# Differences of products 7 and 4 written over their source, and four x operands of the middle groups split in the next stage

## The chip, the cores and the metric

The kernel runs on one core of one Trainium2 chip. Its engines have a queue of instructions each and meet through semaphores: TensorE (PE, matmuls), VectorE (DVE), ScalarE (ACT), GpSimd (POOL) and SyncE (SP, which issues most transfers). The metric is the device time of one execution in microseconds (us); lower is better.

## What is computed

```python
def reference(q, k, v, w_in, w_out):          # q, k, v: 8 x 12 x 448 x 64
    scores = q @ k.transpose(0, 1, 3, 2) / sqrt(64) - log(448)
    a = sigmoid(scores) @ v
    x = a.transpose(0, 2, 1, 3).reshape(3584, 768)
    r = maximum(x @ w_in, 0)                  # w_in: 768 x 2048
    return (r * r) @ w_out                    # w_out: 2048 x 768
```

Everything is float32. Each matmul operand is split in two parts of 32 bits that TensorE takes (fp32r): a high part h, and what is left of the value, the low part l. A product is the sum of three matmuls, h by h, h by l and l by h.

## The kernel before

The attention comes first (to about 236 us). Then the two GEMMs run on the tokens in four groups g = 0 to 3 (WIDTHS: two halves of 512, 512, 512 and 256 tokens each). In each group both GEMMs work by Winograd's form of Strassen's method: a 2x2 block product by seven products of sums, numbered 1 to 7, in place of eight.

**First GEMM** (`gemm1`). A step (n, i) is product n of column block i (of 8), nine matmuls of 128x512. The order of steps is a table: group 0 starts with LEAD, the others go by ROUNDS; all end with TAIL. Products 1, 6, 5 and 3 of a block run on in one PSUM bank ("ha"), 7 and 4 in a second ("hb"), and 2 in a third ("hc"). Product 6 adds to the bank of product 1, so ACT must first copy product 1 out of it: `snap`, L757, tiles "s". By ROUNDS the first steps of a group are (1,0), (2,0), (6,0), (7,0).

The x operands of the next group are made at steps of the second GEMM that the table NEXT_X names, in its products 5, 4 and 3: loads, sums on DVE (L439), and the split by `split_to`, a cast on ACT (L382, "x1h") and a subtraction on DVE (L384, "x1l"). Of 768 rows of x a tile holds 512, and a second one ("y") 256.

**Second GEMM** (`gemm2`). Products come in the order 1, 2, 6, 7, 5, 4, 3, each over four blocks j of the hidden dimension. While a product runs, `operand(n, j)` makes the operands of the next one: a sum on DVE in place (L831 for product 7 in the tile "g11", L834 for product 4 in "g21") and the split in o7_g_j h and l, or o4. In groups 1 and 2, products 2, 7 and 4 are done by the same seven-product method once more. Their operand needs four differences of 128x256 quarters, made by POOL (L846 to L849) in a fresh tile d7_g_j (`differences_of`), which `split_to` then splits in d7_g_j h and l. In names, `d7_1_3l` is product 7, group 1, block 3, low part; the trace leaves numbers in the middle out and shows `d_3l`. For one block PE runs 21 matmuls of 128x256 (L883, "oq") and six of 128x512 ("ob").

What sets the order: attention and the first GEMM of group 0 are in the order in which they are written. From there on a tile scheduler orders each engine's instructions in the build, on all engines at once, and on the chip each engine goes through its own in that order. The pool "op2" has 32 tiles of 128x1024, and all of g, o, d and most x are taken from it.

Of the kernel before, what the change touches and what calls it, by code (L numbers as in the profile page):

```python
# [10 lines left out]
F32R = mybir.dt.float32r  # L11
# [4 lines left out]
ALU = mybir.AluOpType  # L16
# [12 lines left out]
NG = B // 2  # L29
# [11 lines left out]
NG = len(WIDTHS)  # L41
# [28 lines left out]
STEPS = LEAD + [s for s in ROUNDS if s not in LEAD] + TAIL, ROUNDS + TAIL  # L70
# [10 lines left out]
    (4, 4): ("t1", "t2"),  # L81
    (4, 6): (6,),
    (3, 0): ("t3",),
    (3, 1): (7,),
    (3, 3): (5,),
    (3, 5): (3,),
    (3, 6): ("t4",),
    (3, 7): (4,),
}

ORDERS = [(n, i) for n in ORDER for i in range(NI)]
LAST = ORDER[-1], -1
# [3 lines left out]
Q = WIDE // 2  # L96
# [15 lines left out]
def sigmoid_attention_relu2_mlp(  # L112
# [48 lines left out]
    nc = tc.nc  # L161
# [3 lines left out]
    def flat2(name, dtype=F32):  # L165
        return sb.tile([P, 2 * WIDE], dtype, tag="op2", bufs=N2, name=name)
# [9 lines left out]
    def blocks_of(name, n, dtype=F32):  # L176
        return flat2(name, dtype).rearrange("p (a s) -> p a s", s=n)
# [203 lines left out]
    def split_to(hi, lo, raw, later=None):  # L381
        nc.scalar.copy(out=hi, in_=raw)  # L382
        if later is None:
            nc.vector.tensor_sub(out=lo, in0=raw, in1=hi.bitcast(F32))  # L384
        else:
            later.append(lambda: nc.vector.tensor_sub(out=lo, in0=raw, in1=hi.bitcast(F32)))
# [16 lines left out]
    def split_or_joint(raw, name, n):  # L403
        return joint(raw, name, 2 * WIDE // n, n) if n < WIDE else split(raw, name, n)
# [77 lines left out]
    x, vt, xs, at, pav, xo, f64, w = {}, {}, {}, {}, {}, {}, {}, {}  # L482
# [156 lines left out]

    def order_of(g, m):  # L640
        if m == 0:
            return STEPS[g > 0]
        return ORDERS if g < NG - 1 else [*ORDERS[:-NI], LAST]

    sequence = [(g, m, n, i) for g in range(NG) for m in range(2) for n, i in order_of(g, m)]

    def units_of(g, m, n, i):
# [167 lines left out]
    def gemm2(g, blocks, operands1):  # L815
# [3 lines left out]
        ops, t2 = {1: operands1}, {}  # L819
        twice = TWICE if g in TWICE_IN else ()  # L820
        differences = {}

        def operand(n, j):

            if n == 6:
                t2[j] = blocks_of(f"gt2_{g}_{j}", n_tok)
                nc.vector.tensor_sub(out=t2[j], in0=blocks["22", j], in1=blocks["12", j])  # L827
                raw = t2[j]
            elif n == 7:
                raw = blocks["11", j]  # L830
                nc.vector.tensor_sub(out=raw, in0=t2[j], in1=raw)  # L831
            elif n == 4:
                raw = blocks["21", j]
                nc.vector.tensor_sub(out=raw, in0=raw, in1=t2[j])  # L834
            else:
                raw = blocks[{2: "21", 5: "12", 3: "22"}[n], j]
            ops.setdefault(n, {})[j] = split_or_joint(raw, f"o{n}_{g}_{j}", n_tok)
            if n in twice:
                differences[n, j] = differences_of(raw, f"d{n}_{g}_{j}")

        def differences_of(raw, name):

            t, hi, lo = flat2(name), flat2(name + "h", F32R), flat2(name + "l", F32R)
            t1, t2, t3, t4 = (t[:, k * Q : k * Q + Q] for k in range(4))
            b11, b12, b21, b22 = (raw[:, k, h * Q : h * Q + Q] for k in range(2) for h in range(2))
            nc.gpsimd.tensor_tensor(out=t1, in0=b12, in1=b11, op=ALU.subtract)  # L846
            nc.gpsimd.tensor_tensor(out=t2, in0=b22, in1=t1, op=ALU.subtract)
            nc.gpsimd.tensor_tensor(out=t3, in0=b22, in1=b12, op=ALU.subtract)
            nc.gpsimd.tensor_tensor(out=t4, in0=b21, in1=t2, op=ALU.subtract)  # L849
            split_to(hi, lo, t)  # L850
            return hi, lo

        def products(n, j):

            unit = g, 1, j, n
            w, s, d = loaded[unit], summed[unit], differences[n, j]

            def block(e, k):
                return tuple(t[:, k, e * P : e * P + P] for t in w)

            def total(k):
                return tuple(t[:, k * P - P : k * P] for t in s)

            def part(k, h):
                return tuple(t[:, k, h * Q : h * Q + Q] for t in ops[n][j])

            def difference(k):
                return tuple(t[:, k * Q - Q : k * Q] for t in d)

            operands = {  # L870
                2: (block(0, 1), part(1, 0)),
                3: (total(4), part(1, 1)),
                4: (block(1, 1), difference(4)),
                5: (total(1), difference(1)),
                1: (block(0, 0), part(0, 0)),
                6: (total(2), difference(2)),
                7: (total(3), difference(3)),
            }
            for k, ((wh, wl), (xh, xl)) in operands.items():
                at, half = SUMS_AT[k]  # L880
                out = banks["q", at][:, half * Q : half * Q + Q]
                for c, (a, b) in enumerate(((wh, xh), (wh, xl), (wl, xh))):
                    nc.tensor.matmul(  # L883
                        out, a, b, start=j == 0 and c == 0 and half == 0, stop=j == NI // 2 - 1 and c == 2,
                        skip_group_check=True,
                    )
# [71 lines left out]
        def run(n, places):  # L958
            parts = []
            for i, e in places:  # L960
                w = tuple(t[:, i % 2].rearrange("p (c m) -> p c m", m=P) for t in loaded[g, 1, i // 2, n])
                operand = ops[n][i // of]
                x = tuple(t[:, i % of] for t in operand) if n_tok == WIDE else operand[i % of]
                out, first, end = banks[CHAIN[n], e], n in (1, 7, 2) and i == 0, i == NI - 1
                if n_tok < WIDE and (n, e) == (ORDER[-1], NE - 1):
                    out, x = out[:, :n_tok], (x[:, :n_tok], x[:, n_tok:])
                parts.append((out, w, e, x, first, end))
            if isinstance(parts[0][3], tuple):
                for part in parts:
                    product(*part)  # L970
            else:
                side_by_side(parts)
            for i, e in places:
                if i == NI - 1:
                    finish(n, e)
# [19 lines left out]
        def step(n, at):  # L995
            k, i = CHAIN[n], at
            if n in twice:
                if i == 0:
                    for e in range(4):
                        banks["q", e] = bank(f"oq{n}_{g}_{e}", WIDE, 3 if e < 2 else None)  # L1000
                    if n != 4:
                        banks[k, NE - 1] = bank(f"o{k}_{g}", WIDE)
                j = i // 2
                if i == 2 * j:
                    products(n, j)
                else:
                    for c in range(2):
                        w = tuple(t[:, c].rearrange("p (c m) -> p c m", m=P) for t in loaded[g, 1, j, n])
                        x = tuple(t[:, c] for t in ops[n][j])
                        product(banks[k, NE - 1], w, NE - 1, x, n != 4 and (j, c) == (0, 0), (j, c) == (NI // 2 - 1, 1))  # L1010
                if i == NI - 1:
                    finish_twice(n)
                after = ORDER.index(n) + 1
                if after < len(ORDER) and i % of == 0:
                    operand(ORDER[after], i // of)
                return
# [11 lines left out]
            if after < len(ORDER) and i % of == 0:  # L1028
                operand(ORDER[after], i // of)
# [3 lines left out]
    def run_steps(begin, end, between):  # L1033
        for at in range(begin, end):
            g, m, n, i = sequence[at]
            if (m, n, i) == (0, *order_of(g, 0)[0]):
                made[g] = gemm1(g, ops[g])
            if (m, n, i) == (1, *ORDERS[0]):
                step, blocks, operands, done = made[g]
                done()  # L1040
                second[g] = gemm2(g, blocks, operands)
            (second[g] if m else made[g][0])(n, i)
            for piece in between.get(at, ()):
                piece()
            for piece, unit in stream.get(at, ()):
                piece(unit)
            if m and g < NG - 1:
                if (n, i) == next(iter(NEXT_X)):
                    ops[g + 1], next_x[g] = x_operands(g + 1)
                for name in NEXT_X.get((n, i), ()):  # L1050
                    next_x[g][name]()

    made, second, next_x = {}, {}, {}

# [95 lines left out]
```

## Time and profile before

| | |
|---|---|
| median of three runs | 1070.48 us (1066.46 to 1071.03) |
| profiled execution | 1069.48 us, its span 1067.7 us |
| mean granted TensorE clock | 0.995 |
| busy: PE, DVE, ACT, POOL | 1051.8, 835.4, 687.9, 241.7 us |

The span goes from the first to the last instruction; the execution's own time is 1.8 us longer. The view of the waits tells for how long an engine stood still, and which engine's instruction ended that. The timeline tells where it stood. In a timeline the microseconds of an instruction are from its start to its end, whatever holds it up in between.

### The profile page before, as it was taken

The numbers are of one execution on the slowest core, as the hardware profiler recorded it, in microseconds if no ns is written. First come the engines' busy times: TensorE is split into PE (matmuls) and PEld (weight loads), VectorE is DVE, ScalarE is ACT, GpSimd is POOL, SyncE is SP. The second block draws the span as 40 slices with busy tenths as digits, with TensorE's granted clock in tenths as the row PEclk, the third lists the DMA queues.
The fourth block names the chain that finished last, engine by engine and source line by source line (L and its number), as shares of the span: only waits on it lengthen the run. The fifth ranks groups of instructions, "written<-read, shape, count | busy, mean of one in ns | idle before, by whom it ended". The sixth has DMA issues, their size and how long they took to land.

```text
span 1067.7 us, 17202 instructions
## 1 busy us (share of the span) xinstructions
PE 1051.8 (99%) x6418; PEld 821.5 (77%) x6418; DVE 835.4 (78%) x1045; ACT 687.9 (64%) x960; POOL 241.7 (23%) x188
## 2 busy tenths in 40 slices
PE   9999999999999999999999999989999999999998
PEld 4555555557888888877888888878888887889987
DVE  5999998977768899793555698894556689877897
ACT  7998998877667855663334647473344647567863
POOL 1322231300222344300000639300002559100000
PEclk9999999999999999998999999999999999999999
DMA  9999999983666787983334868862336778775662
GB/s 363 395 371 392 335 404 361 336 286 116 214 208 207 245 285 241 331 297 116 102 91 140 297 205 298 288 230 75 103 96 218 251 258 286 258 242 165 203 209 69
DMA packets 121874, 255.93 MB, mean 240 GB/s; under 512 B 11712, under 2 KB 63680, under 8 KB 121792
## 3 DMA queue, kind: packets, MB, share of 16 engines
q1 hardware_dynamic: 121648, 254.79, 69.7%
q8 instruction: 50, 0.82, 0.3%
q14 instruction: 32, 0.26, 0.1%
q10 hardware_dynamic: 144, 0.07, 0.0%
HBM read 193.46 MB, written 61.34 MB: 239 GB/s over the span
## 4 chain that ended last, share of the span: by engine, by line
PE 81%; DVE 9%; DMA 3%; ACT 2%; POOL 2%; issue 2%; SPq 0%; ACTq 0%; DVEq 0%; POOLq 0%
PE ha L626 20%; PE oa L626 14%; PE pav L356 11%; PE hb L626 9%; PE sc L325 9%; PE hc L626 4%; PE oq L883 3%; PE ob L626 3%; PE oc L626 2%; DMA w<-w 2%; PE sr L341 2%; PE pav L368 2%; DVE w L384 1%; POOL d L846 1%; DVE gt L827 1%
## 5 line engine op out<-in xcount | busy, mean ns | idle before, releaser
L384 DVE TENSOR_TENSOR w<-w 128x768 fp32r<-128x768 f32 (+1 forms) x164 | 148.5, 913 | 95.7 <-ACT w L382 82.1
L382 ACT CAST w<-w 128x768 fp32r<-128x768 f32 (+1 forms) x165 | 127.0, 778 | 82.4 <-DMA w<-w 78.8
L313 ACT ACTIVATE at<-sc 128x896 f32<-128x896 f32 x144 | 119.3, 941 | 3.8 <-PE sc L325 3.7
L356 PE MATMUL pav<-at,v 64*64 64x448 f32 x1152 | 118.1, 540 | 0.0
L846 POOL TENSOR_TENSOR d<-g 128x256 f32<-128x256 f32 x24 | 33.6, 1400 | 339.2 <-PE ha L626 283.7
L215 POOL TENSOR_TENSOR a<-a,f 128x768 int32<-128x768 int32 x24 | 52.8, 2201 | 159.4 <-DVE a L212 94.0
L356 PEld LDWEIGHTS pav<-at,v 64*64 64x64 f32 x1152 | 41.6, 133 | 60.8 <-issue 53.5
L757 ACT COPY s<-ha 128x512 f32<-128x512 f32 (+1 forms) x64 | 34.0, 533 | 81.9 <-PE ha L626 77.8
L592 DVE TENSOR_TENSOR ql<-x,qh 128x896 fp32r<-128x896 f32 x46 | 67.9, 1516 | 0.0
L690 ACT CAST w<-w 128x768 fp32r<-128x768 f32 x56 | 46.7, 834 | 29.6 <-DMA w<-w 29.6
L325 PE MATMUL sc<-qh 64*128 64x448 f32 x282 | 53.9, 379 | 0.0
L325 PE MATMUL sc<-ql,qh 64*128 64x448 f32 x282 | 51.3, 360 | 0.0
L325 PE MATMUL sc<-qh,ql 64*128 64x448 f32 x282 | 51.0, 358 | 0.0
L378 DVE TENSOR_TENSOR xo<-pav,xo 128x448 f32<-128x448 f32 x48 | 29.5, 621 | 25.2 <-ACT xo L374 25.0
L626 PE MATMUL ha<-x_1h,w 128*128 128x512 f32 x128 | 45.7, 398 | 3.0 <-ACT s L757 3.0
L626 PE MATMUL ha<-x_2h,w 128*128 128x512 f32 x128 | 45.7, 398 | 2.8 <-ACT s L757 2.8
L215 POOL TENSOR_TENSOR b<-b,fd 128x384 int32<-128x384 int32 x16 | 20.4, 1278 | 118.8 <-ACT w L382 56.9
L626 PE MATMUL oa<-o_0h,w 128*128 128x512 f32 x144 | 46.3, 389 | 0.0
L626 PE MATMUL oa<-o_1h,w 128*128 128x512 f32 x144 | 46.3, 389 | 0.0
L626 PE MATMUL oa<-o_2h,w 128*128 128x512 f32 x144 | 46.3, 389 | 0.0
L626 PE MATMUL oa<-o_3h,w 128*128 128x512 f32 x144 | 46.3, 389 | 0.0
L626 PE MATMUL ha<-x_0h,w 128*128 128x512 f32 x128 | 44.8, 390 | 0.0
(575 smaller groups left out, 3057.0 us busy)
## 6 DMA issues: line engine op xcount, KB each, us to landing
w<-w SPq DMA_DIRECT2D x192, 384.0 KB, 3.7
w<-h SPq DMA_DIRECT2D x56, 384.0 KB, 5.6
x<-qk SPq DMA_DIRECT2D x47, 448.0 KB, 6.2
f<-w_in SPq DMA_DIRECT2D x16, 768.0 KB, 8.7
v<-v SPq DMA_DIRECT2D x24, 448.0 KB, 6.6
xd<-xo SPq DMA_DIRECT2D x48, 224.0 KB, 4.8
h<-w SPq DMA_DIRECT2D x28, 384.0 KB, 4.3
w<-s SPq DMA_DIRECT2D x48, 192.0 KB, 7.2
```

The source lines that it names most:

```text
L215: nc.gpsimd.tensor_tensor(out=wb, in0=wb, in1=t.bitcast(I32)[:, :, 0], op=ALU.add)
L313: nc.scalar.activation(at, sc, AF.Sigmoid, bias=NEG_LOG_S, scale=SCALE)
L325: nc.tensor.matmul(sc[:, j], x[kp][rows, 1, ks], x[qp][rows, 0], start=(n == 0), stop=(n == len(passes) - 1),)
L356: nc.tensor.matmul(sums[columns, h], vt[rows, n % 2 * NT + t, columns], at[t][rows, j], start=(t == 0 and (n % 2, h) != (1, 1)), stop=(t = ...
L382: nc.scalar.copy(out=hi, in_=raw)
L384: nc.vector.tensor_sub(out=lo, in0=raw, in1=hi.bitcast(F32))
L592: nc.vector.tensor_sub(out=xs[n][1], in0=x[n], in1=xs[n][0].bitcast(F32))
L626: nc.tensor.matmul(out, a[:, c], b, start=first and n == 0, stop=last and n == 2, skip_group_check=True)
L690: nc.scalar.copy(out=hi, in_=hi.bitcast(F32))
L757: nc.scalar.copy(out=s, in_=banks[chain, i])
L846: nc.gpsimd.tensor_tensor(out=t1, in0=b12, in1=b11, op=ALU.subtract)
L883: nc.tensor.matmul(out, a, b, start=j == 0 and c == 0 and half == 0, stop=j == NI // 2 - 1 and c == 2, skip_group_check=True,)
```

## The change

There are two parts.

First, `differences_of` gets an argument `spent`. For products 7 and 4 it is true: the four differences are written over their own source, the tile g11 (product 7) or g21 (product 4), and no fresh tile d is taken. The order is now t1, t3, t2, t4, and they lie in the tile as t1, t3, t4, t2, so that each is written where the source is no longer needed; `difference(k)` picks them accordingly. Since the source is overwritten, POOL's first write to a block now has to come after both instructions that read that block for the split: ACT's cast o7_g_j h and DVE's subtraction o7_g_j l. Each of the four POOL instructions now follows the one before it. Product 2 keeps its fresh tile.

Second, in groups 1 and 2 the steps of the first GEMM take the order of group 0: (1,0), (2,0), (1,1), (2,1), (6,0), (7,0), (6,1), (5,0), (7,1), (3,0) and so on. Their x operands 7, 5, 3 and 4 (with the sum t4 for the last) are now made at steps 0, 1, 3, 5 and 6 of this order (EARLY_X), no longer in product 3 of the second GEMM before. Group 3 keeps its order and the old places (LATE_X).

```diff
@@ -81,12 +81,9 @@
     (4, 4): ("t1", "t2"),
     (4, 6): (6,),
     (3, 0): ("t3",),
-    (3, 1): (7,),
-    (3, 3): (5,),
-    (3, 5): (3,),
-    (3, 6): ("t4",),
-    (3, 7): (4,),
 }
+EARLY_X = {0: (7,), 1: (5,), 3: (3,), 5: ("t4",), 6: (4,)}
+LATE_X = {(3, 1): (7,), (3, 3): (5,), (3, 5): (3,), (3, 6): ("t4",), (3, 7): (4,)}
 
 ORDERS = [(n, i) for n in ORDER for i in range(NI)]
 LAST = ORDER[-1], -1
@@ -639,7 +636,7 @@
 
     def order_of(g, m):
         if m == 0:
-            return STEPS[g > 0]
+            return STEPS[g == NG - 1]
         return ORDERS if g < NG - 1 else [*ORDERS[:-NI], LAST]
 
     sequence = [(g, m, n, i) for g in range(NG) for m in range(2) for n, i in order_of(g, m)]
@@ -836,18 +833,20 @@
                 raw = blocks[{2: "21", 5: "12", 3: "22"}[n], j]
             ops.setdefault(n, {})[j] = split_or_joint(raw, f"o{n}_{g}_{j}", n_tok)
             if n in twice:
-                differences[n, j] = differences_of(raw, f"d{n}_{g}_{j}")
-
-        def differences_of(raw, name):
-
-            t, hi, lo = flat2(name), flat2(name + "h", F32R), flat2(name + "l", F32R)
-            t1, t2, t3, t4 = (t[:, k * Q : k * Q + Q] for k in range(4))
-            b11, b12, b21, b22 = (raw[:, k, h * Q : h * Q + Q] for k in range(2) for h in range(2))
+                differences[n, j] = differences_of(raw, f"d{n}_{g}_{j}", n != 2)
+
+        def differences_of(raw, name, spent):
+
+            hi, lo = flat2(name + "h", F32R), flat2(name + "l", F32R)
+            flat = raw.rearrange("p k s -> p (k s)")
+            to = flat if spent else flat2(name)
+            b11, b12, b21, b22 = (flat[:, n * Q : n * Q + Q] for n in range(4))
+            t1, t3, t4, t2 = (to[:, n * Q : n * Q + Q] for n in range(4))
             nc.gpsimd.tensor_tensor(out=t1, in0=b12, in1=b11, op=ALU.subtract)
+            nc.gpsimd.tensor_tensor(out=t3, in0=b22, in1=b12, op=ALU.subtract)
             nc.gpsimd.tensor_tensor(out=t2, in0=b22, in1=t1, op=ALU.subtract)
-            nc.gpsimd.tensor_tensor(out=t3, in0=b22, in1=b12, op=ALU.subtract)
             nc.gpsimd.tensor_tensor(out=t4, in0=b21, in1=t2, op=ALU.subtract)
-            split_to(hi, lo, t)
+            split_to(hi, lo, to)
             return hi, lo
 
         def products(n, j):
@@ -865,7 +864,8 @@
                 return tuple(t[:, k, h * Q : h * Q + Q] for t in ops[n][j])
 
             def difference(k):
-                return tuple(t[:, k * Q - Q : k * Q] for t in d)
+                at = (1, 3, 4, 2).index(k) * Q
+                return tuple(t[:, at : at + Q] for t in d)
 
             operands = {
                 2: (block(0, 1), part(1, 0)),
@@ -1049,6 +1049,11 @@
                     ops[g + 1], next_x[g] = x_operands(g + 1)
                 for name in NEXT_X.get((n, i), ()):
                     next_x[g][name]()
+                for name in LATE_X.get((n, i), ()) if g == NG - 2 else ():
+                    next_x[g][name]()
+            if m == 0 and 0 < g < NG - 1:
+                for name in EARLY_X.get(at - sequence.index((g, 0, *order_of(g, 0)[0])), ()):
+                    next_x[g - 1][name]()
 
     made, second, next_x = {}, {}, {}
```

The build is ordered anew by this. On DVE, in the second GEMM of group 1 at product 7, this stood before (L384 is the split's subtraction, L831 and L834 the sums for products 7 and 4):

```order
L384 TENSOR_TENSOR o7_1_0l_6457<-g11_1_0_5340,o7_1_0h_6456 128x1024
L831 TENSOR_TENSOR g11_1_3_5906<-gt2_1_3_6408,g11_1_3_5906 128x1024
L384 TENSOR_TENSOR d7_1_0l_6462<-d7_1_0_6460,d7_1_0h_6461 128x1024
L384 TENSOR_TENSOR o7_1_1l_6497<-g11_1_1_5506,o7_1_1h_6496 128x1024
L834 TENSOR_TENSOR g21_1_1_5658<-g21_1_1_5658,gt2_1_1_6334 128x1024
L384 TENSOR_TENSOR d7_1_1l_6502<-d7_1_1_6500,d7_1_1h_6501 128x1024
L384 TENSOR_TENSOR o7_1_2l_6537<-g11_1_2_5699,o7_1_2h_6536 128x1024
L834 TENSOR_TENSOR g21_1_2_5851<-g21_1_2_5851,gt2_1_2_6371 128x1024
L834 TENSOR_TENSOR g21_1_3_6054<-g21_1_3_6054,gt2_1_3_6408 128x1024
L384 TENSOR_TENSOR d7_1_2l_6542<-d7_1_2_6540,d7_1_2h_6541 128x1024
L384 TENSOR_TENSOR o7_1_3l_6579<-g11_1_3_5906,o7_1_3h_6578 128x1024
L384 TENSOR_TENSOR d7_1_3l_6584<-d7_1_3_6582,d7_1_3h_6583 128x1024
```

and now, where the split's line is L381 and the sums' are L828 and L831:

```order
L381 TENSOR_TENSOR o7_1_0l_6457<-g11_1_0_5312,o7_1_0h_6456 128x1024
L828 TENSOR_TENSOR g11_1_3_5906<-gt2_1_3_6408,g11_1_3_5906 128x1024
L831 TENSOR_TENSOR g21_1_1_5658<-g21_1_1_5658,gt2_1_1_6334 128x1024
L831 TENSOR_TENSOR g21_1_2_5851<-g21_1_2_5851,gt2_1_2_6371 128x1024
L381 TENSOR_TENSOR d7_1_0l_6461<-g11_1_0_5312,d7_1_0h_6460 128x1024
L381 TENSOR_TENSOR o7_1_1l_6496<-g11_1_1_5480,o7_1_1h_6495 128x1024
L831 TENSOR_TENSOR g21_1_3_6054<-g21_1_3_6054,gt2_1_3_6408 128x1024
L381 TENSOR_TENSOR d7_1_1l_6500<-g11_1_1_5480,d7_1_1h_6499 128x1024
L381 TENSOR_TENSOR o7_1_2l_6535<-g11_1_2_5699,o7_1_2h_6534 128x1024
L381 TENSOR_TENSOR d7_1_2l_6539<-g11_1_2_5699,d7_1_2h_6538 128x1024
L381 TENSOR_TENSOR o7_1_3l_6576<-g11_1_3_5906,o7_1_3h_6575 128x1024
L381 TENSOR_TENSOR d7_1_3l_6580<-g11_1_3_5906,d7_1_3h_6579 128x1024
```

The split o7_1_1l now stands behind d7_1_0l, o7_1_2l behind d7_1_1l, and o7_1_3l behind d7_1_2l, each directly, as before; but before, POOL did not have to wait for any of them. The input of a d split is now the tile g11 itself.

On DVE at product 4 of group 1, from the splits of product 5 on, before:

```order
L384 TENSOR_TENSOR o5_1_1l_6670<-g12_1_1_5629,o5_1_1h_6669 128x1024
L384 TENSOR_TENSOR o5_1_2l_6705<-g12_1_2_5822,o5_1_2h_6704 128x1024
L384 TENSOR_TENSOR o5_1_3l_6740<-g12_1_3_6084,o5_1_3h_6739 128x1024
L384 TENSOR_TENSOR o4_1_0l_6781<-g21_1_0_5465,o4_1_0h_6780 128x1024
L384 TENSOR_TENSOR d4_1_0l_6786<-d4_1_0_6784,d4_1_0h_6785 128x1024
L384 TENSOR_TENSOR o4_1_1l_6821<-g21_1_1_5658,o4_1_1h_6820 128x1024
L900 TENSOR_TENSOR qe7_1_6749<-oq7_1_2_6610,qe7_1_6749 128x256
L901 TENSOR_TENSOR qt7_1_6750<-oq7_1_3_6611,qe7_1_6749 128x256
L902 TENSOR_TENSOR qe7_1_6749<-oq7_1_1_6609,qe7_1_6749 128x256
L384 TENSOR_TENSOR d4_1_1l_6826<-d4_1_1_6824,d4_1_1h_6825 128x1024
```

and now (L900 to L918 combine what product 7 left in PSUM, L949 forms an output):

```order
L381 TENSOR_TENSOR o4_1_0l_6777<-g21_1_0_5491,o4_1_0h_6776 128x1024
L902 TENSOR_TENSOR qe7_1_6745<-oq7_1_1_6605,qe7_1_6745 128x256
L904 TENSOR_TENSOR q7_1_0_6751<-oq7_1_0_6604,qe7_1_6745 128x512
L907 TENSOR_TENSOR q7_1_1_6752<-oq7_1_1_6605,qt7_1_6746 128x256 x2
L918 TENSOR_TENSOR t2_1_0_6572<-t2_1_0_6572,q7_1_0_6751 128x512
L918 TENSOR_TENSOR t2_1_1_6596<-t2_1_1_6596,q7_1_1_6752 128x512
L381 TENSOR_TENSOR d4_1_0l_6781<-g21_1_0_5491,d4_1_0h_6780 128x1024
L381 TENSOR_TENSOR o4_1_1l_6816<-g21_1_1_5658,o4_1_1h_6815 128x1024
L381 TENSOR_TENSOR d4_1_1l_6820<-g21_1_1_5658,d4_1_1h_6819 128x1024
L381 TENSOR_TENSOR o4_1_2l_6855<-g21_1_2_5851,o4_1_2h_6854 128x1024
L949 TENSOR_TENSOR o22_1_0_6900<-oa_1_0_6110,q7_1_0_6751 128x512
L381 TENSOR_TENSOR d4_1_2l_6859<-g21_1_2_5851,d4_1_2h_6858 128x1024
```

The o4 splits stand behind the d4 splits of the block before them here as well, and d4_1_0l is behind the combination of product 7.

On ACT, at the start of group 1's first GEMM (w: weights, o12: outputs of group 0, s1_1_0: the copy of product 1 for block 0), before:

```order
L382 CAST w0_1_0_2_5254<-w0_1_0_2_5254 128x768
L382 CAST x4_1h_5308<-x21_1_4942 128x1024
L382 CAST w0_1_1_1_5287<-w0_1_1_1_5287 128x768
L951 COPY o12_0_0_5284<-oa_0_0_4289 128x512
L382 CAST w0_1_0_3_5342<-w0_1_0_3_5342 128x384
L951 COPY o12_0_1_5300<-oa_0_1_4290 128x512
L951 COPY o12_0_2_5303<-oa_0_2_4291 128x512
L382 CAST y4_1h_5310<-yx21_1_4943 128x512
L757 COPY s1_1_0_5326<-ha_1_0_5316 128x512
```

and now:

```order
L379 CAST w0_1_1_0_5203<-w0_1_1_0_5203 128x768
L379 CAST w0_1_0_1_5226<-w0_1_0_1_5226 128x768
L379 CAST w0_1_1_1_5249<-w0_1_1_1_5249 128x768
L379 CAST w0_1_0_2_5263<-w0_1_0_2_5263 128x768
L951 COPY o12_0_0_5260<-oa_0_0_4289 128x512
L951 COPY o12_0_1_5274<-oa_0_1_4290 128x512
L379 CAST w0_1_2_0_5316<-w0_1_2_0_5316 128x768
L951 COPY o12_0_2_5277<-oa_0_2_4291 128x512
L754 COPY s1_1_0_5292<-ha_1_0_5282 128x512
```

The casts x4_1h and y4_1h, which stood ahead of the copy s1_1_0, now come after it, with those of x5, x3, y3, y5 and y7. On DVE in the same GEMM, the sum g22_1_0 (L761 before), which takes product 5 out of the bank "ha" for product 3, stood directly behind the split of the weight tile w0_1_2_1; two more splits, y4_1l and that of w0_1_1_3, now stand between them. At the start of group 3, ACT's copy s1_3_0 now stands behind the casts of x4_3 and of one more weight tile.

## Rows read from the trace of the kernel before

**Rows 1.** The page's first part: busy us of an engine, its share of the span, and instructions.

```profile
PE 1051.8 (99%) x6418; PEld 821.5 (77%) x6418; DVE 835.4 (78%) x1045; ACT 687.9 (64%) x960; POOL 241.7 (23%) x188
```

**Rows 2.** The view of the waits, PE's alone, over the whole span: who waited for whom, us in total, times, longest.

```profile
PE ha L626 <- ACT s L757: 7.2, 3, 3.0
PE oq L883 <- DVE d_3l L384: 2.0, 2, 1.0
PE oq L883 <- DVE d_2l L384: 1.5, 2, 0.9
```

**Rows 3.** Timeline of PE at the start of group 1's first GEMM (its first matmul in the first row): start us, us, engine and line, output<-inputs, and in brackets the idle time before and what ended it. Matmuls overlap; how far apart they are is the difference of two starts.

```profile
474.23 0.39 PE L626 MATMUL ha<-x_1h,w 128*128 128x512 f32 x1
...
481.45 0.79 PE L626 MATMUL ha<-x_1h,w 128*128 128x512 f32 x1 [2.99 <-ACT s L757]
...
484.18 0.63 PE L626 MATMUL ha<-y_1h,w 128*128 128x512 f32 x1
484.61 0.63 PE L626 MATMUL ha<-y_1l,w 128*128 128x512 f32 x1
...
487.17 0.47 PE L626 MATMUL hb<-x_1l,w 128*128 128x512 f32 x1
...
487.71 0.40 PE L626 MATMUL hb<-y_1h,w 128*128 128x512 f32 x1
487.95 0.40 PE L626 MATMUL hb<-y_1l,w 128*128 128x512 f32 x1
```

**Rows 4.** Windows over all engines: the stretch in us from the span's start, its length, busy us and instructions of PE, PEld, DVE, ACT and POOL, the granted TensorE clock, the DMA share and GB/s.

```profile
482.00:488.00 6.00, 6.00 (x17) 4.66 (x16) 2.46 (x3) 2.15 (x3) 0.00 (x0) 0.56 0.41 161
...
716.00:720.00 4.00, 3.43 (x9) 2.76 (x10) 4.00 (x6) 1.35 (x3) 0.00 (x0) 0.57 0.33 126
```

**Rows 5.** Timeline of PE at the start of group 2's first GEMM.

```profile
716.57 0.79 PE L626 MATMUL ha<-x_2h,w 128*128 128x512 f32 x1 [2.79 <-ACT s L757]
...
719.29 0.47 PE L626 MATMUL ha<-y_2h,w 128*128 128x512 f32 x1
```

**Rows 6.** Timeline of ACT at the start of group 1's first GEMM.

```profile
476.42 1.04 ACT L382 CAST x_1h<-x 128x1024 fp32r<-128x1024 f32 x1
...
479.94 0.63 ACT L382 CAST y_1h<-yx 128x512 fp32r<-128x512 f32 x1
480.82 0.59 ACT L757 COPY s<-ha 128x512 f32<-128x512 f32 x1 [0.25 <-DMA outT<-o]
```

**Rows 7.** Timeline of DVE in group 1's first GEMM.

```profile
492.51 0.96 DVE L384 TENSOR_TENSOR w<-w 128x768 fp32r<-128x768 f32 x1 [4.46 <-ACT w L382]
493.38 0.68 DVE L761 TENSOR_TENSOR g<-s,ha 128x512 f32<-128x512 f32 x1
```

**Rows 8.** Timeline of POOL in the second GEMM: the differences of product 7 in group 1 (625 to 655 us), the first of product 4 (655.11), and the first block of product 7 in group 2 (869.75 on).

```profile
625.35 1.33 POOL L846 TENSOR_TENSOR d<-g 128x256 f32<-128x256 f32 x1 [10.82 <-PE oq L883]
...
637.07 1.29 POOL L846 TENSOR_TENSOR d<-g 128x256 f32<-128x256 f32 x1 [6.32 <-DVE o_0l L384]
638.33 1.72 POOL L848 TENSOR_TENSOR d<-g 128x256 f32<-128x256 f32 x1
...
641.80 1.60 POOL L849 TENSOR_TENSOR d<-g,d 128x256 f32<-128x256 f32 x1
...
654.42 0.73 POOL L849 TENSOR_TENSOR d<-g,d 128x256 f32<-128x256 f32 x1
655.11 0.74 POOL L846 TENSOR_TENSOR d<-g 128x256 f32<-128x256 f32 x1
...
869.75 5.00 POOL L846 TENSOR_TENSOR d<-g 128x256 f32<-128x256 f32 x1 [6.03 <-DVE o_0l L384]
...
875.41 0.74 POOL L847 TENSOR_TENSOR d<-g,d 128x256 f32<-128x256 f32 x1
876.22 0.74 POOL L849 TENSOR_TENSOR d<-g,d 128x256 f32<-128x256 f32 x1
```

**Rows 9.** Timeline of DVE beside them, in product 7 of group 1.

```profile
635.42 1.21 DVE L384 TENSOR_TENSOR o_0l<-g,o_0h 128x1024 fp32r<-128x1024 f32 x1
...
637.69 1.75 DVE L384 TENSOR_TENSOR d_0l<-d,d_0h 128x1024 fp32r<-128x1024 f32 x1
...
656.27 1.35 DVE L384 TENSOR_TENSOR d_3l<-d,d_3h 128x1024 fp32r<-128x1024 f32 x1 [2.52 <-ACT d_3h L382]
```

**Rows 10.** Timeline of ACT in the same stretch.

```profile
651.53 0.85 ACT L690 CAST w<-w 128x768 fp32r<-128x768 f32 x1
655.19 1.05 ACT L382 CAST d_3h<-d 128x1024 fp32r<-128x1024 f32 x1 [2.80 <-POOL d L849]
```

**Rows 11.** Timeline of PE in group 1's second GEMM: the first matmul of blocks 0 and 1 of product 7, the wait for product 7's last differences, the first matmul of products 5 and 4, and the first use of the low part of product 4's last differences.

```profile
642.75 0.28 PE L883 MATMUL oq<-o_0h,w 128*128 128x256 f32 x1
...
646.65 0.28 PE L883 MATMUL oq<-o_1h,w 128*128 128x256 f32 x1
...
657.68 0.38 PE L883 MATMUL oq<-d_3l,w 128*128 128x256 f32 x1 [1.01 <-DVE d_3l L384]
...
660.84 0.39 PE L626 MATMUL oa<-o_0h,w 128*128 128x512 f32 x1
...
677.16 0.28 PE L883 MATMUL oq<-o_0h,w 128*128 128x256 f32 x1
...
689.69 0.28 PE L883 MATMUL oq<-d_3l,w 128*128 128x256 f32 x1
```

## The prediction

> **What bounds the kernel now.** First the page's busy times: PE works 1051.8 of 1067.7 us [rows 1], so a change can win only what PE stands still or runs slowly, and it loses whatever it makes PE wait. Then the waits of PE: 7.2 us in three waits for ACT's copy "s", and 2.0 and 1.5 us in two each for the last low parts of the product 7 differences [rows 2]. Then the timelines around these waits. At the start of group 1's first GEMM PE waits 2.99 us, and then its matmuls are 0.43 us apart until 487.17, where they later are 0.24 [rows 3]; the granted clock of that window is 0.56 [rows 4], so this is the lower of the two levels, 1.2 in place of 2.4 GHz. 5.7 us at 0.43 are 13 matmuls, of which each lost about 0.2: 2.7 us. At the start of group 2 the same happens after 2.79 us, from 716.57 to 719.29 [rows 5], clock 0.57 [rows 4]: 6 or 7 matmuls, 1.3 us. So the places that the change aims at hold 2.99 + 2.7 = 5.7 us (group 1), 2.79 + 1.3 = 4.1 us (group 2) and 3.5 us (product 7), 13.3 in all. That is the most that it can bring.
>
> **Differences in place: the new wait.** PE wants a new block every 3.9 us (642.75 to 646.65, [rows 11]). Before, POOL needed only the sum in g11 and a free tile: its first differences of product 7 ran from 625.35, ten microseconds before the split o7_1_0l, which begins at 635.42 [rows 8, 9]. Even so the last ones came 1.01 us late [rows 11]. Now POOL may write block j only behind o7_1_jl on DVE. DVE's order has o7_1_1l directly behind d7_1_0l, which needs the cast d7_1_0h, which needs POOL's block 0; and so on. The four blocks, which could run ahead, become one loop: POOL, ACT, DVE, DVE, POOL. What is queued behind DVE's wait for d7_1_0h is o7_1_1l, and POOL's next block waits for just that.
>
> Prices of the loop. A POOL quarter alone takes 0.74 us, and one that follows on another starts 0.81 after it (875.41, 876.22): a block alone is 3 x 0.81 + 0.74 = 3.2. Beside DVE a quarter takes up to 1.72, and a block 6.3 (637.07 to 641.80 + 1.60) [rows 8]. ACT's cast takes 1.05 and DVE's split 1.21 (1.75 beside POOL) [rows 9, 10]. Hand-overs are 0.03 to 0.06: POOL ends at 655.15, ACT starts at 655.19, DVE at 656.27, PE at 657.68 [rows 8 to 11]. From POOL's end of a block to its next start: cast 1.05, the next cast o7h (starts 0.95 later), split 1.21 and hand-overs, 3.4 us; where a copy (0.5) or a weight cast (0.85, of which 0.74 counts since the next one overlaps, [rows 10]) stands between the two casts, 3.85 and 4.1.
>
> Product 7 of group 1, by ACT's and DVE's new order. o7_1_0l ends at 636.63; without POOL's early differences beside the work ahead of it I let it end 0.75 earlier, 635.9. Block 0 has three DVE sums beside it, 6.3, and 0.15 to start: 642.4. Loop 3.4: 645.8. Block 1, one DVE sum beside it, 3.2 + 1.0: 650.0. Loop 3.85: 653.9. Block 2, 3.2: 657.1. Loop 4.1: 661.2. Block 3, 3.2: 664.4. Cast and split, 2.3: 666.7. PE got this part at 657.68 [rows 11]: **9.1 us later**.
>
> Product 4. Product 5 (16.3 us, 660.84 to 677.16, [rows 11]) slides by 9.1 and ends at 686.3. In ACT's order three weight casts, four o5 casts and a copy, together 7.2 us, stand between d7_1_3h (done at 665.5) and the end of o4_1_0h; with its split, 674.0. Before, POOL had begun product 4 at 655.11 [rows 8]. Now block 0 takes 4.5 (the combination of product 7 beside it), and then 3.35, 3.2, 3.35, 3.2, 4.1, 4.2 and 2.3 follow as above: 702.3. PE used that part at 689.69 [rows 11]: 12.6 us later, so product 4 adds 3.5 to the 9.1. The later product 3 hides nothing, since PE is busy through it. **Group 1: +12.6.** Group 2 has the same order; its stalls of before were a little longer in the second place (1.5 for two, [rows 2]), so I take **+12**.
>
> Block 0 beside DVE can also go otherwise: in group 2 one quarter took 5.00 us and the next ones 0.74 each [rows 8], 7.2 for the block, 0.9 more than the 6.3 taken. The Trainium skill ("SBUF — State Buffer", section "Who interferes with whom") says that a DVE instruction with two SBUF inputs and a GpSimd one that reads SBUF exclude each other, and that the second to issue blocks until the first finishes. By that rule a quarter would lose at most one DVE instruction, and the 5.00 shows one that lost a whole run of them; with the rule the forecast stays, with the row in both groups it is 1.8 higher.
>
> **Clock.** The new waits in product 7 are about 1, 3.7, 3 and 3 us long, so some reach the 2.8 to 3.0 us behind which the clock fell [rows 3 to 5]. Slow matmuls ahead of a next wait cost nothing, since the chain sets it. After the last wait of product 4 nothing hides them: 1.3 to 2.7, and I take **+2 a group, 4**. Bounds: 0 and 2.7 for each of four last waits.
>
> **The operands moved to the next stage.** By the order of group 0, two more steps stand ahead of (6,0); a step is nine matmuls, 2.04 us (72 of them take the 16.32 of product 5, [rows 11]). So PE comes to it at 474.23 + 4 x 2.04 = 482.4 in place of 478.3. The copy s1_1_0 began at 480.82, with x4_1h (1.04) and y4_1h (0.63) ahead of it in ACT's queue [rows 6]; these go behind it. It is there in time and the wait is gone, with the slow matmuls behind it. What is late next: (3,0) at 474.23 + 9 x 2.04 = 492.6 needs g22_1_0 on DVE. Before, the split of w0_1_2_1 started at 492.51, held by its cast, and g22_1_0 at 493.38 [rows 7]. I let the weight tile come no earlier; two more splits stand between, and g22_1_0 ends about 494.2: 1.6 us of waiting (0 if the weights come earlier, 3 if both new splits come late). **Group 1: 5.7 - 1.6 = -4.1. Group 2**, by the same working with 1.2 left: **-2.9**. In the second GEMM the casts removed from product 3 free ACT and DVE, which do not bound PE there: 0. Group 3 keeps its table, but the copy s1_3_0 now stands behind two casts of x4_3 (0.63 at most each, [rows 6]) and one weight cast (0.85, [rows 10]): **+2**, bounds 0 and 2.1. The 16 tiles that are no longer taken free nothing that PE waits for in [rows 2]: 0.
>
> **Sum**, against the profiled execution's 1069.48 us (1.0 below the median): 12.6 + 12 + 4 + 2 - 4.1 - 2.9 = +23.6, so **1093**.
>
> **Rivals.** First, *it works as meant* and ends faster. POOL alone needs 3.2 us a block, PE 3.9, so if DVE did o7_1_1l to o7_1_3l ahead of the d7 splits, POOL would run its blocks in a row. The differences would come in time and 9.8 (starts of the groups) to 13.3 us would go: 1056 to 1060. For it: ACT and DVE stand idle for 2.5 us and more around these very instructions [rows 9, 10]. Against: DVE takes its instructions in order, and o7_1_1l is behind d7_1_0l. It decides at a loop under 3.9 us; mine is 6.6 to 7.3. Second, *the chain is bare*: no DVE instruction ever holds POOL up. Product 7 ends at 635.9 + 4 x 3.2 + 3 x 3.4 + 2.3 = 661.2, 3.5 late, product 4 is hidden by product 5: +7 for both groups, against -7 to -9.8 at the starts and up to 4 elsewhere: 1067 to 1073. Against it: three DVE sums stand beside block 0. Third, *the clock falls and stays*: each of the four last waits of products 7 and 4 costs 2.7 in full (+6.8 over the 4 taken), or the starts of the groups aren't repaired at all (+7); both, +14: 1100 to 1107.
>
> **How the numbers follow.** The forecast, the loop with 1078 to 1100 by its bounds, 0.72; as meant 0.07; bare chain 0.08; clock or starts worse 0.13. The range of 1078 to 1105 takes in the forecast and most of the third rival. A measurement of this kernel can tell about 0.5% (5.4 us) from no change: faster 0.08, same 0.06 (1065 to 1076), slower 0.86.
>
> **What would show it.** In the timeline after, POOL's first differences of product 7 start behind o_0l at about 636, not ten microseconds ahead; POOL's blocks are 6.6 to 7.5 us apart with idle time ended by DVE o_1l, o_2l, o_3l; PE's waits for d_1l, d_2l and d_3l in products 7 and 4 sum to some 12 to 16 us a group; the waits for "s" at 481 and 717 are gone, with a wait of 1 to 3 us for DVE's g22 in their place. If PE's waits for the differences stay under 2 us a group, the step "one loop" is wrong; if they are there and the time is far from 1093, the clock or the starts of the groups are mis-sized.

## The result, and the profile after

The changed kernel took 1084.24 us in the median (1084.08 to 1085.11, 4 runs) against 1068.64 for the kernel before: the ratio is 1.0147, 95% interval 1.0119 to 1.0176. It is slower by 1.5%. Its profiled execution took 1084.13 us. The page gives its span, and PE's busy time:

```profile
span 1082.4 us, 17191 instructions
...
PE 1057.4 (98%) x6418; PEld 824.7 (76%) x6418; DVE 818.1 (76%) x1045; ACT 686.1 (63%) x960; POOL 209.2 (19%) x188
```

The span is 14.7 us longer than before; PE's busy time is 5.6 us longer [rows 1], the rest is waiting. The waits of PE over the whole span (who waited for whom, us in total, times, longest):

```profile
PE oq L883 <- ACT d_1h L379: 4.7, 2, 2.3
PE oq L883 <- ACT d_3h L379: 3.7, 3, 2.0
PE oq L883 <- DVE d_3l L381: 3.5, 4, 0.9
PE oq L883 <- ACT d_2h L379: 1.9, 2, 1.7
PE oq L883 <- DVE d_0l L381: 1.8, 2, 0.9
PE oq L883 <- DVE d_1l L381: 1.8, 2, 0.9
PE oq L883 <- DVE d_2l L381: 1.7, 2, 0.9
PE ha L623 <- ACT s L754: 1.4, 2, 1.1
```

The copy "s" took 7.2 us in three waits before [rows 2]; 1.4 us are left. In its place the waits for the differences d take 19.1 us (3.5 before): 8.8 us in group 1 and 10.2 in group 2, by the rows of PE's timeline. PE now often waits twice for a block, first for the high part, which ACT's cast makes, and then for the low part, which DVE makes. This is block 1 of product 7 in group 1:

```profile
645.06 0.38 PE L883 MATMUL oq<-d_1h,w 128*128 128x256 f32 x1 [2.32 <-ACT d_1h L379]
646.32 0.38 PE L883 MATMUL oq<-d_1l,w 128*128 128x256 f32 x1 [0.88 <-DVE d_1l L381]
```

PE goes on as soon as the cast is there, does one matmul, and waits another 0.88 us for the subtraction: the two are one wait of 3.2 us.

How long each stage took is read from the timeline of PE, as the time between the first matmuls of two stages. A wait at the start of a stage is therefore counted in the stage before it:

| stage | before | after | difference | forecast |
|---|---|---|---|---|
| group 1, first GEMM | 120.28 | 114.40 | -5.88 | -4.1 |
| group 1, products 1, 2, 6 | 48.24 | 48.24 | 0 | 0 |
| group 1, product 7 | 18.09 | 28.66 | +10.57 | +9.1 |
| group 1, product 5 | 16.32 | 16.32 | 0 | 0 |
| group 1, products 4 and 3 | 31.92 | 33.87 | +1.95 | +3.5, and clock +2 |
| group 2, first GEMM | 118.69 | 114.65 | -4.04 | -2.9 |
| group 2, products 1, 2, 6 | 48.24 | 48.24 | 0 | 0 |
| group 2, product 7 | 18.38 | 27.21 | +8.83 | |
| group 2, products 5, 4, 3 | 48.24 | 52.50 | +4.26 | +12 with product 7, and clock +2 |
| group 3, first GEMM | 61.37 | 61.62 | +0.25 | +2 |
| ahead of group 1; group 3's second GEMM to the end | | | -0.26; -0.98 | 0 |

The loop is there, block by block. POOL in product 7 of group 1 (the first, sometimes the last quarter of each block; start, us, what ended the idle time before):

```profile
629.93 3.92 POOL L845 TENSOR_TENSOR g<-g 128x256 f32<-128x256 f32 x1 [21.39 <-DVE o_0l L381]
...
635.57 0.74 POOL L848 TENSOR_TENSOR g<-g 128x256 f32<-128x256 f32 x1
639.86 1.65 POOL L845 TENSOR_TENSOR g<-g 128x256 f32<-128x256 f32 x1 [3.55 <-DVE o_1l L381]
...
643.21 0.72 POOL L848 TENSOR_TENSOR g<-g 128x256 f32<-128x256 f32 x1
647.77 0.73 POOL L845 TENSOR_TENSOR g<-g 128x256 f32<-128x256 f32 x1 [3.84 <-DVE o_2l L381]
...
655.03 0.73 POOL L845 TENSOR_TENSOR g<-g 128x256 f32<-128x256 f32 x1 [4.10 <-DVE o_3l L381]
```

Each block after the first waits 3.55 to 4.10 us for the split o_1l, o_2l or o_3l, and then takes 3.2 us (block 1, with a DVE instruction beside it, 4.1). Before, POOL had done block 0 ahead of the split o_0l [rows 8, 9]. ACT and DVE in between:

```profile
636.34 1.05 ACT L379 CAST d_0h<-g 128x1024 fp32r<-128x1024 f32 x1 [9.98 <-POOL g L848]
637.29 1.04 ACT L379 CAST o_1h<-g 128x1024 fp32r<-128x1024 f32 x1
```

```profile
628.63 1.22 DVE L381 TENSOR_TENSOR o_0l<-g,o_0h 128x1024 fp32r<-128x1024 f32 x1
629.77 1.22 DVE L828 TENSOR_TENSOR g<-gt,g 128x1024 f32<-128x1024 f32 x1
630.90 2.36 DVE L831 TENSOR_TENSOR g<-g,gt 128x1024 f32<-128x1024 f32 x2
637.42 1.23 DVE L381 TENSOR_TENSOR d_0l<-g,d_0h 128x1024 fp32r<-128x1024 f32 x1 [4.16 <-ACT d_0h L379]
638.56 1.22 DVE L381 TENSOR_TENSOR o_1l<-g,o_1h 128x1024 fp32r<-128x1024 f32 x1
...
659.31 1.23 DVE L381 TENSOR_TENSOR d_3l<-g,d_3h 128x1024 fp32r<-128x1024 f32 x1 [4.36 <-ACT d_3h L379]
```

POOL ends block 0 at 636.31; ACT's d_0h runs from 636.34, and o_1h only behind it; d_0l runs from 637.42; o_1l from 638.56 to 639.78; POOL goes on at 639.86. ACT stood idle for 9.98 us ahead of d_0h with o_1h behind it, and DVE for 4.16 us ahead of d_0l with o_1l behind it. d_3l ends at 660.54, 30.7 us after o_0l (629.85); the forecast had 30.8, from 635.9 to 666.7.

Clock, by windows (stretch, length, busy us of PE, PEld, DVE, ACT and POOL, granted clock, DMA share, GB/s):

```profile
480.00:500.00 20.00, 20.00 (x90) 16.34 (x89) 13.51 (x18) 12.08 (x19) 0.00 (x0) 1.00 0.39 108
647.00:651.00 4.00, 4.00 (x17) 3.49 (x16) 0.70 (x1) 1.19 (x3) 2.92 (x4) 0.57 0.13 49
661.00:665.00 4.00, 4.00 (x18) 3.72 (x18) 3.55 (x4) 4.00 (x6) 0.00 (x0) 0.57 0.02 4
896.00:900.00 4.00, 4.00 (x18) 3.42 (x17) 0.79 (x1) 0.27 (x1) 2.90 (x4) 0.57 0.00 0
937.00:941.00 4.00, 3.96 (x17) 3.75 (x18) 3.56 (x4) 4.00 (x7) 0.00 (x0) 0.57 1.06 395
```

At the start of group 1 the granted clock is now 1.00, where it was 0.56 [rows 4]. Behind some of the waits of products 7 and 4 it is 0.57 in the windows shown.

### The profile page after: what moved, and what is told of

The parts are those of the page before. It is cut to its first block, busy times and chain, and to the rows that moved or that the text cites. A ratio compares the mean times of both kernels' runs of the same rounds, so it can differ in the third digit from the quotient of the medians.

```text
span 1082.4 us, 17191 instructions
## 1 busy us (share of the span) xinstructions
PE 1057.4 (98%) x6418; PEld 824.7 (76%) x6418; DVE 818.1 (76%) x1045; ACT 686.1 (63%) x960; POOL 209.2 (19%) x188
## 5 line engine op out<-in xcount | busy, mean ns | idle before, releaser
L381 DVE TENSOR_TENSOR w<-w 128x768 fp32r<-128x768 f32 (+1 forms) x164 | 148.8, 915 | 82.0 <-ACT w L379 72.1
L845 POOL TENSOR_TENSOR d<-g 128x256 f32<-128x256 f32 x8 | 9.1, 1139 | 286.0 <-DVE g L758 136.2
L687 ACT CAST w<-w 128x768 fp32r<-128x768 f32 x56 | 46.5, 833 | 20.2 <-PE ha L623 10.0
```

The lines of the kernel that those rows point to most:

```text
L687: nc.scalar.copy(out=hi, in_=hi.bitcast(F32))
```

## The experiments

All but one keep the moved x operands (`EARLY_X`). In the short diffs, - is the changed kernel and + the experiment.

**Fresh tiles, moved operands.**

```diff
-                differences[n, j] = differences_of(raw, f"d{n}_{g}_{j}", n != 2)
+                differences[n, j] = differences_of(raw, f"d{n}_{g}_{j}", False)
```

> The x operands in the new places, the differences of products 7 and 4 in fresh tiles as before. Theory (the loop POOL, ACT, DVE, DVE of the in-place differences costs all of the loss, the moved operands only gain): products 7 and 4 of the middle groups go back to 18.1 to 18.4 and 15.6 us, the first GEMMs of groups 1 and 2 stay at 114.4 and 114.6 us, and the time is 1084.2 - 25 = about 1059 us. Rival (the moved operands need tiles or queue time that only the in-place differences free): the fresh tiles come late, PE waits in product 7, 4 or at the group starts for more than 5 us, and the time stays above 1066 us.

Measured: 1059.24 us, ratio 0.9922 (0.9892 to 0.9951): faster than the kernel before and the changed one. First GEMMs of groups 1 and 2: 114.3 and 114.2 us; product 7: 18.77 and 18.18; product 4: 15.60 twice. PE's waits:

```profile
PE oq L883 <- DVE d_3l L381: 2.0, 2, 1.0
PE oq L883 <- DVE d_2l L381: 1.9, 2, 1.3
PE ha L623 <- ACT s L754: 1.4, 1, 1.4
```

The waits for d are those of before, to 0.4 us. The moved operands need nothing that only the in-place differences free; the rival is out.

**In place, operands where they were.**

```diff
-            return STEPS[g == NG - 1]
+            return STEPS[g > 0]
-                for name in LATE_X.get((n, i), ()) if g == NG - 2 else ():
+                for name in LATE_X.get((n, i), ()):
-            if m == 0 and 0 < g < NG - 1:
+            if False:
```

> The differences of products 7 and 4 in place, the x operands in the places of before. Theory (loop): products 7 and 4 take 27 to 29 and 17 to 20 us as in the changed kernel, the group starts have their waits of 2.8 to 3.0 us for the copy s back, and the time is 1084.2 + 10 = about 1094 us. Rival (part of the loss comes from the moved operands): about 1080 us or less.

Measured: 1095.83 us, ratio 1.0272 (1.0239 to 1.0304). Product 7 took 28.70 and 29.19 us, product 4 17.10 and 15.68. The waits for "s" are back, and longer than before:

```profile
PE ha L623 <- ACT s L754: 10.8, 3, 4.1
```

The two parts nearly add up: -9.4 us for the operands alone and +27.2 for the differences alone make +17.8, where +15.6 was measured. They are not quite independent: with the operands in their old places the in-place differences lengthened the waits for "s" by 3.6 us (10.8 in place of 7.2).

**In place, each block's differences written behind the next block's split.** Nothing else of the loop is changed: only the order in which the program asks for the work. The scheduler then puts o_1h ahead of d_0h on ACT, and o_1l ahead of d_0l on DVE.

```diff
-                differences[n, j] = differences_of(raw, f"d{n}_{g}_{j}", n != 2)
+                if n == 2: differences[n, j] = differences_of(raw, ..., False)
+                else:
+                    waiting.append((n, j, raw))
+                    if j > 0: take_differences()           # of block j - 1
+                    if j == NI // 2 - 1: take_differences()
```

> As the changed kernel, but the in-place differences of block j are written in the program behind the split of block j + 1, so that on DVE o7_1l stands ahead of d7_0l, o7_2l ahead of d7_1l and so on. Theory (the loop, by the order on DVE, costs the time): POOL's blocks follow each other about every 4 us, the last difference of product 7 comes some 3 us late in place of 11, product 4 has no wait, and the time is 1060 to 1065 us. Rival (writing in place is slow by itself, since POOL starts only behind o_0l and its four instructions are a chain): 1080 us or more.

Measured: 1074.27 us, ratio 1.0061 (1.0037 to 1.0085). Neither theory had this time. Product 7 is as the theory has it: 20.85 and 20.92 us, 2.8 and 2.5 more than before. But PE waited 2.9 and 0.9 us at the start of product 3 for the weights' cast (ACT w L687). These waits make up all but 0.2 us of what product 4 took above 15.60 (18.76 and 16.74); product 4 itself had no wait for differences. Product 3 took 19.83 us in group 1; behind the wait its matmuls ran at the lower clock from 694.9 to 701.6 (granted clock 0.50 from 695 to 701), which cost 2.7 us.

**Only product 4 in place.**

```diff
-                differences[n, j] = differences_of(raw, f"d{n}_{g}_{j}", n != 2)
+                differences[n, j] = differences_of(raw, f"d{n}_{g}_{j}", n == 4)
```

> As the changed kernel, but only product 4's differences in place and product 7's in fresh tiles. Theory (loop, beginning behind o4_0l, which is split some 11 us before product 4 begins): product 7 has its 18.1 to 18.4 us back, and product 4's four blocks take 27.6 us from o4_0l on, so its last difference is about 4 us late in each group: about 1059 + 8 to 10 = 1067 to 1069 us. Rival (product 4's waits in the changed kernel are only what product 7 handed on): no wait in product 4, about 1059 us.

Measured: 1076.93 us, ratio 1.0090 (1.0057 to 1.0123), some 8 us more than the theory. PE, at the end of product 4 and the start of product 3 in group 1:

```profile
687.31 0.39 PE L883 MATMUL oq<-o_3h,w 128*128 128x256 f32 x1 [2.22 <-ACT w L687]
...
697.26 0.79 PE L623 MATMUL oa<-o_0h,w 128*128 128x512 f32 x1 [4.25 <-ACT w L687]
```

It waits for weights here, not for differences. The first wait is still the loop's: the weights of block 3 had landed at 671.86, but on ACT their cast (686.43) stood behind the cast d_3h, which waited for POOL:

```profile
685.48 1.04 ACT L379 CAST d_3h<-g 128x1024 fp32r<-128x1024 f32 x1 [4.73 <-POOL g L848]
```

The second wait comes by another way. On DVE the output o22 (L949) of product 5, whose sum had long been complete, stood behind d_3l:

```profile
686.55 1.23 DVE L381 TENSOR_TENSOR d_3l<-g,d_3h 128x1024 fp32r<-128x1024 f32 x1 [4.37 <-ACT d_3h L379]
687.70 0.68 DVE L949 TENSOR_TENSOR o<-oa,q 128x512 f32<-128x512 f32 x1
```

and on SP's queue its store stood ahead of the loads of product 3's weights (the last row):

```profile
688.41 0.34 SPq L952 DMA_DIRECT2D outT<-o  x1
...
690.31 0.38 SPq L284 DMA_DIRECT2D w<-w  x1
```

```profile
SPq L952 <- DVE o L949: 20.3, 3, 19.6
```

The last row is from the view of the waits of SP's queue, 660 to 700 us: one wait of 19.6 us for DVE's o. In the kernel with fresh tiles the same two rows come 12 to 13 us earlier:

```profile
675.48 0.34 SPq L952 DMA_DIRECT2D outT<-o  x1
...
677.92 0.61 SPq L284 DMA_DIRECT2D w<-w  x1
```

(Product 4 itself began 1.7 us earlier there.) So the late last block is paid twice, at product 4 and through SP at product 3. In group 2 PE waited 1.7 us for the last differences and 2.5 us for the weights of product 3.

**The same, with o22's stores issued from POOL's queue.**

```diff
-            nc.sync.dma_start(out=to, in_=o)
+            queue = nc.gpsimd if name == "22" and g in TWICE_IN else nc.sync
+            queue.dma_start(out=to, in_=o)
```

> As the run with only product 4 in place, but the stores of product 5's outputs o22 in the middle groups are issued from POOL's queue and not from SP's. Theory (the late split d4_3l holds o22 on DVE, its store holds SP's queue, and the loads of product 3's weights stand behind it): the loads go out some 10 us earlier, PE's waits for w at the start of product 3 (4.3 and 2.5 us) go, with the slow clock after them, and 3 to 5 us a group remain for the late d4_3l: about 1066 us. Rival (the weights are late for another reason, such as a tile that is not free): PE waits for w as before, about 1077 us.

Measured: 1075.90 us, ratio 1.0078 (1.0055 to 1.0101). In group 2 the wait for w at the start of product 3 went, as the theory had it. In group 1 a wait of 3.9 us stayed. The waits of SP's queue name the next one in line:

```profile
SPq L428 <- DVE o L949: 14.6, 1, 14.6
```

A load of x (L428) now waits for DVE's o, and the weights are behind that. But the first of them, issued at 687.95, had landed at 691.83, and its cast ran at 695.03 only. On ACT it stood behind a split of x, which waited for the moved store:

```profile
692.61 0.62 ACT L379 CAST y_2h<-yx 128x512 fp32r<-128x512 f32 x1 [5.28 <-DMA outT<-o]
```

So o22, late on DVE, held the weights by two more ways, the load on SP's queue and the cast on ACT; moving the store alone helps against neither. (4.0 us of waiting for "s" at the start of group 3 took back most of what group 2 had won.)

**Only product 4 in place, its last differences written behind product 5's outputs.**

```diff
-                differences[n, j] = differences_of(raw, f"d{n}_{g}_{j}", n != 2)
+                waiting.append((n, j, raw))
+                if not (n == 4 and j == NI // 2 - 1): take_differences()
...
             i = at
+            if (n, i) == (5, NI - 1) and waiting: take_differences()
```

> As the run with only product 4 in place, but the differences of product 4's last block are written in the program behind product 5's outputs, so that on DVE o22 stands ahead of d4_3l and not behind it. Theory (whatever on SP waits for o22 is held as long as DVE waits for d4_3h): o22 is done some 6 us earlier, the loads of product 3's weights go out as much earlier, PE's wait for w at the start of product 3 shrinks from 4.3 us to under 1.5 and the slow clock behind it goes; about 4 us a group remain for the late d4_3l: 1066 to 1069 us. Rival (the weights wait for something else): 1075 us or more.

Measured: 1072.16 us, ratio 1.0037 (1.0019 to 1.0054). PE has no wait for w any more. But the time is 3 us above the theory. The largest part is one row, of the waits of PE from 670 to 700 us:

```profile
PE oq L896 <- DVE d_3l L381: 3.9, 1, 3.9
```

d_3l now stood behind an x sum (L436) as well, which waited for its load and ran at 687.60. Behind this wait the matmuls ran at the lower clock until 697.3 (granted clock 0.50 from 691 to 697), which cost 2.8 us more. In group 2, without that sum, the wait for d_3l is 0.9. The first GEMM of group 1 also took 2.2 us more than with fresh tiles (116.49 us), 1.3 of it in waits for "s" and g22.

**Both in place, late, and o22 first.** The two orders together.

```diff
+                if n == 2: take_differences()
+                elif j > 0:
+                    take_differences()                      # of block j - 1
+                    if n == 7 and j == NI // 2 - 1: take_differences()
...
             i = at
+            if (n, i) == (5, NI - 1) and waiting: take_differences()
```

> Products 7 and 4 in place, each block's differences written one block later, and product 4's last ones behind product 5's outputs. Theory (two orders on DVE make all of the loss: o7l and o4l behind d of the block before, and o22 behind d4_3l): product 7 takes 20.9 us, no wait for w, 1065 to 1067 us. Rival (writing product 4 in place costs otherwise too): about 1074 us as the run with both late.

Measured: 1065.80 us, ratio 0.9972 (0.9961 to 0.9983), as the theory had it. On ACT and DVE the splits of block 1 now stand ahead of the differences of block 0 (product 7 of group 1; d_0h runs at 636.47):

```profile
626.38 1.05 ACT L379 CAST o_1h<-g 128x1024 fp32r<-128x1024 f32 x1
```

```profile
629.88 1.22 DVE L381 TENSOR_TENSOR o_1l<-g,o_1h 128x1024 fp32r<-128x1024 f32 x1
...
637.55 1.47 DVE L381 TENSOR_TENSOR d_0l<-g,d_0h 128x1024 fp32r<-128x1024 f32 x1 [4.18 <-ACT d_0h L379]
```

POOL there (where block 0 ends and block 1 begins, and where block 2 ends and block 3 begins):

```profile
635.69 0.74 POOL L861 TENSOR_TENSOR g<-g 128x256 f32<-128x256 f32 x1
636.39 0.74 POOL L858 TENSOR_TENSOR g<-g 128x256 f32<-128x256 f32 x1
...
644.56 1.60 POOL L861 TENSOR_TENSOR g<-g 128x256 f32<-128x256 f32 x1
646.12 1.73 POOL L858 TENSOR_TENSOR g<-g 128x256 f32<-128x256 f32 x1
```

The blocks follow each other without a pause, though all are written in place. PE's waits:

```profile
PE oq L896 <- DVE d_0l L381: 2.3, 2, 1.1
PE oq L896 <- DVE d_2l L381: 1.8, 2, 0.9
PE oq L896 <- DVE d_3l L381: 1.8, 2, 0.9
PE oq L896 <- DVE d_1l L381: 1.4, 2, 0.7
```

No wait for w, and 7.3 us for differences. Of the 6.6 us that remain against fresh tiles, 4.9 are in product 7 (20.86 and 20.94 us, where fresh tiles take 18.77 and 18.18), whose first block POOL can begin only behind o_0l.

**Only product 7 in place,** and **the same with its differences late**.

```diff
-                differences[n, j] = differences_of(raw, f"d{n}_{g}_{j}", n != 2)
+                differences[n, j] = differences_of(raw, f"d{n}_{g}_{j}", n == 7)
```

In the second, product 7's call goes through `waiting` as in the run with both late.

> As the changed kernel, but only product 7's differences in place and product 4's in fresh tiles. Theory (product 7's loop is late by itself; product 4 in fresh tiles starts on POOL as soon as product 7's blocks are done and is hidden by product 5): product 7 takes 27 to 29 us as in the changed kernel, product 4 has its 15.6 us back, and the time is 1059.2 + 9.9 + 9.0 = about 1078 us. Rival (the late product 7 makes product 4 late too, whatever tile it writes): product 4 keeps 17 to 20 us, about 1084 us.

> Product 7's differences in place, written in the program one block later, product 4's in fresh tiles. Theory (loop, by the order on DVE): product 7 takes 20.9 us as in the run with both late, 2.1 and 2.7 more than with fresh tiles, nothing is late behind it, about 1064 us. Rival (writing in place costs by itself): 1075 us or more.

Measured: 1080.49 us, ratio 1.0117 (1.0081 to 1.0153), and 1065.41 us, ratio 0.9971 (0.9953 to 0.9990). Product 7 took 29.78 and 28.49 us in the first, 21.01 and 20.91 in the second; product 4 had its 15.6 to 15.7 us in both. The order in which the program asks for the work is worth 15 us. It changes the order of ACT (o_1h ahead of d_0h) and of DVE (o_1l ahead of d_0l) together; no run changed one of the two alone.

## Why the prediction was right, and where its sizes were off

Slower was right, and so was the cause: "the four blocks, which could run ahead, become one loop". The block time (3.2 us alone), the ways from POOL to POOL (3.4, 3.85 and 4.1 in the forecast; 3.55, 3.84 and 4.10 on the chip) and the length of the chain (30.8 and 30.7) were measured nearly as worked out. That the order of the splits on ACT and DVE makes the loop is shown by the runs that change that order and leave the in-place writes as they are. The forecast named DVE's order; on ACT o_1h stands behind d_0h too (637.29), which it counted among the prices only. Two of its signs were off: PE's waits for the differences sum to 8.8 and 10.2 us a group, not 12 to 16, and POOL's blocks started 9.9, 7.9 and 7.3 us apart, not 6.6 to 7.5 (the forecast's own times give 9.7, 8.1 and 7.3).

Of 1093 forecast and 1084.13 of the profiled execution, 9 us are off:

- **Products 7, 5, 4 and 3 of both groups**, with the clock: forecast 28.6, measured 25.6. From the start of product 7 on, PE first used the low part of product 4's last differences 12.0 us later than before in group 1 and 11.5 in group 2, for 12.6 and 12 in the forecast. What came behind that was put at 2 us a group for the clock, and measured 0.5 and 1.6; so the clock, +4, is the term that was mis-sized most. Behind product 4 it fell in group 2 only (937 to 941). The slow stretch behind product 7's last wait (661 to 665) did lengthen product 7 by some 1.5 us, but product 4's chain on POOL, ACT and DVE ran on meanwhile, so that its wait was shorter: group 1 paid 10.6 us in product 7 for 9.1, and 2.0 in products 4 and 3 for 3.5.
- **The starts of groups 1 and 2**: forecast -7.0, measured -9.9, 0.1 more than the 9.8 that the forecast counted in these places. The wait of (3,0) for g22, put at 1.6 us, did not come: "0 if the weights come earlier" was the case. The other runs that keep the moved operands had it at 0 to 1.0 us.
- **The start of group 3**: forecast +2, measured +0.25. The copy s1_3_0 was delayed, but (6,0) waited 1.1 us where it had waited 1.4.
- **Around the groups**: -1.2, not forecast; the wait of 0.8 us for o_1j, which PE had in the second GEMM of group 3, is gone. Nothing was tried on this.

The rival that it works as meant was out by the order, which is where the forecast put the decision: with o_l ahead of d_l, and o22 ahead of product 4's last differences, the kernel in place ran in 1065.8 us, not slower than before. The price that the rival gave (1056 to 1060) was too low, since POOL still has to begin behind o_0l. The rival of a bare chain had 25.3 us from o_0l to d_3l. Its blocks 2 and 3 were right, 3.2 us each, but block 0 lost 3.2 and block 1 0.9 us to DVE's instructions beside them, and the ways from POOL to POOL were 1.3 us longer in all.

One thing the prediction missed does not show in the changed kernel, only in the run with product 4 alone: what is queued behind the d splits on DVE (o22), behind that on SP (weights), and behind the d casts on ACT (weights again). In the changed kernel the scheduler happens to put the first o22 ahead of d4_2l and the others ahead of d4_3l.

Left open: why the scheduler puts o22 at different places on DVE in these builds, what ACT's order and DVE's order are worth each by itself, and where the 0.8 us in group 3's second GEMM went.

## What to carry to other kernels

Writing a result over its source frees a tile but adds a wait for the source's last reader; before doing it, look where that reader stands in its engine's queue. If the last reader of block j + 1 stands behind something that needs the result of block j, the blocks have become a loop through all engines, and its length, not the busiest engine, sets the time; asking for the reads one block ahead, on every engine that reads, undoes it. Split a change of two parts and time each: here one part was worth -9.4 us and the other +27.2.

## What was not expected of the hardware

A POOL instruction that meets a run of DVE subtractions can lose to all of them. The first quarter of product 7 took 3.92 us (629.93) beside three back-to-back DVE instructions, the last of which ends at 633.26 (629.77, 630.90); before, it took 5.00 us [rows 8] beside a run of four, which ends at 874.16; alone it takes 0.74. At other places POOL and DVE alternated, 1.6 to 1.7 us a quarter, as in the run with both late (644.56, 646.12). The Trainium skill ("SBUF — State Buffer", section "Who interferes with whom") calls the ports that the two share an exclusive lock; by these rows the one that waits can stay locked out over a run of instructions. For the forecast it made no difference, since block 0 took 6.4 us where 6.3 had been put.

The same wait did not always bring the clock down. PE waited 3.2 us at block 1 of product 7 in both groups; in group 1 a stretch at half clock began at 647, right behind, in group 2 none did until 896, behind block 2's wait of 2.6 us. In product 4 of group 2 the clock fell behind a wait of 2.2 us (937), in group 1 not at all behind waits of 1.0 us in all.
